# Feed-forward blocks of four pairs of chunks in a fused block-attention and FFN kernel, with rooms in SBUF shared anew

## Chip, cores and metric

The kernel runs on one core of a Trainium2 chip. The metric is the device time of one execution in microseconds (us). Before the change the median of three runs is 938.62 us (938.25 to 939.14), so differences under about 0.2% (1.9 us) can't be told from no change.

## What is computed

Queries, keys and values are float32 of 8 batches, 8 heads, 576 positions and 64 values per head. A sequence is cut into 9 chunks of 64 positions, and a chunk attends to itself alone. The result, laid out as 4608 tokens of 512 values, goes through a feed-forward network (FFN) with a squared ReLU:

```python
scores = scale * np.matmul(q_c, k_c.transpose(0, 1, 2, 4, 3))
scores = scores - np.max(scores, axis=-1, keepdims=True)
attn = np.exp(scores)
attn = attn / (np.sum(attn, axis=-1, keepdims=True) + 1e-09)
out = np.matmul(attn, v_c)
...
h = x @ w_in
r = np.maximum(h, 0.0)
g = r * r
return (g @ w_out).astype(np.float32)
```

The weights (512 by 2048 and 2048 by 512) arrive as float64, as pairs of 32-bit words.

## The kernel before, in words

**Values in two parts.** Every float32 value that a large matrix product uses is split into a high part, which fits the type fp32r, and a low part, the rest. A product is then three matmuls: high times high, high times low, low times high. In the FFN the names are `xh`, `xl` (tokens), `wi` (first weights), `gh`, `gl` (squared ReLU) and `wo` (second weights).

**Pairs, units and blocks.** A pair is two neighbouring chunks, 128 tokens; there are 36. A unit is one pair with four of the eight heads, so there are 72 units, two to a pair (unit u belongs to pair u // 2). Pairs are grouped into FFN blocks by the list `blocks` (line 63): one of four pairs, ten of three, one of two. For a block of n pairs the FFN goes in 16 steps f, one for each 128 of the 2048 hidden values. A step has 12 matmuls into the PSUM tile `h` (`mm_in`, L623: four quarters of the 512 inputs, three matmuls each, moving operand n*128 wide), then `act` (ReLU on ACT, square on DVE, high part on ACT, low part on DVE), and, two steps later (`LAG`), three matmuls for each pair into the PSUM tiles `o` (`mm_out`, L667, moving operand 512 wide). The accumulators `o` of a block are taken in turn from four PSUM banks. At a block's end each is copied to an SBUF tile `ob` (two buffers) and stored.

**Attention of the late pairs.** The first 8 pairs (`NN`) are done in the first stage by other code, while the weights are converted. Each of the other 28 goes through these steps, for a pair or for its two units:
- `load_qk`: 16 DMAs bring q and k of a pair into the tiles `q_raw` and `k_raw`, one buffer each. `transpose_pair` (L284) turns them on DVE into `qt` and `kt` and then calls for the next pair's load.
- `stack_qk` (L297): the high part of q goes to the tile `qst` on ACT (L306), the low part to a tile `ql` on DVE (L308), and a DMA on each half copies it into the other half of `qst` (L310). High and low parts of k go to `kst` (L312, L316), with two DMAs (L314). `qst` and `kst` have one buffer each.
- `s2`: four matmuls `sc` (L353) into two PSUM tiles, copied by ACT and added by DVE (L363, L365) to `e`; then maximum, difference, exponential. `norm` divides by the sum.
- `s3`: two transposes `pt` on PE (L403), then `pst` on ACT (L417), two DMAs (L419) and the low parts on DVE (L421).
- `load_v` and `stack_v`: four DMAs of 64 by 8 by 64 values bring v of a whole pair into two tiles `v_raw` (L278, two buffers in all); ACT and POOL split each unit's part into `vs` (L331, L334). After the pair's second unit the next pair's v is called for.
- `s4`: four matmuls `xt` (L437) into two PSUM tiles, whose sums `x` become columns of `xh` and `xl` (L449 to L457).

`sc`, `pt` and `xt` share two PSUM banks in turn.

**What sets the order.** All DMAs of the late pairs and the stores are issued by SP, one after the other; an issue that has to wait holds up those behind it. The order on PE is written out in lines 935 to 959: the matmuls and `act` calls of a block (`ops`) are cut into as many equal pieces as there are slots, and `merge` spreads a slot's attention steps over its piece. Slot t holds `s2` of unit t-1, `s4` of t-3, `stack_v` of t-2, `norm` of t-1, `transpose_pair` and `stack_qk` for unit t if it opens a pair, and `s3` of t-2. Block 1 (the second) also opens the late tiles and has two slots without attention first; then its slots run from t = 16 until the pairs of block 2 are through. Any later block's slots bring the pairs of the block behind it. The other engines' order is set by a scheduler from the order of the code and priorities.

**The first stage.** `first_block` lists the work of block 0, the conversion of the weights and the attention of pairs 0 to 7 with costs, and a small planner (`Plan`) sorts it. Pair 7 belongs to block 2 there, whose `xh` and `xl` use the room of block 0's, so its result is placed by `place(NN - 1)` at the end of the stage. The copies `kt` of these pairs lie in the pool `nat`.

Of the kernel before, what the change touches and what calls it, by code (L numbers as in the profile page):

```python
# [10 lines left out]
F32 = mybir.dt.float32  # L11
F32R = mybir.dt.float32r
# [8 lines left out]
def kernel(  # L21
# [24 lines left out]
    P = 128  # L46
# [13 lines left out]

    ABUFS = 3
    PRIO = 300
    blocks = [4] + [3] * 10 + [2]
    LAG = 2
    HEAD = 1
    REST = 0
# [7 lines left out]
    XB = (max(blocks[::2]), max(blocks[1::2]))  # L74


    NN = sum(blocks[:2]) + 1
    first_pair = [sum(blocks[:b]) for b in range(len(blocks))]

    const = ctx.enter_context(tc.tile_pool(name="const", bufs=1))  # L80
# [29 lines left out]
    def open_late():  # L110

        early.close()
        pool = ctx.enter_context(tc.tile_pool(name="late", bufs=2))
        late["pool"] = pool
        late["q"] = pool.tile([P, H, 2, CH], F32R, name="qst", tag="qst", bufs=1)
        late["p"] = pool.tile([P, 2, HP, 2, 2, CH], F32R, name="pst", tag="pst", bufs=1)
        load_v(NN)
        nc.gpsimd.memset(late["p"].bitcast(F32), 0.0)
        late["k"] = pool.tile([P, 2, 2, H, CH], F32R, name="kst", tag="kst", bufs=1)
        for c in range(2):  # L120
            r = slice((1 - c) * CH, (2 - c) * CH)
            nc.gpsimd.memset(late["k"].bitcast(F32)[r, 1, c], 0.0)
# [133 lines left out]
                        s = src[bb, :, i0:i0 + 32, dh * 32:(dh + 1) * 32]  # L256
                        nc.sync.dma_start(out=t[r0:r0 + 32, :, ih, :], in_=s.rearrange("h i d -> i h d"))

    def load_v(pair):


        if pair < NN:
            for c in range(2):
                bb, n0 = divmod(2 * pair + c, NCH)
                for h2, r in enumerate(halves):
                    s = v[bb, h2:H:2, n0 * CH:(n0 + 1) * CH, :]
                    nc.sync.dma_start(
                        out=vbd[slot_of(pair)][r, :, c, h2, :], in_=s.rearrange("h i d -> i h d")
                    )
            return  # L270
        pairs[pair]["v"] = []
        for c in range(2):
            t = late["pool"].tile([P, H, D], F32, name=f"v_raw{pair}_{c}", tag="v_raw")
            pairs[pair]["v"].append(t)
            bb, n0 = divmod(2 * pair + c, NCH)
            s = v[bb, :, n0 * CH:(n0 + 1) * CH, :].rearrange("h i d -> i h d")
            for r in halves:
                nc.sync.dma_start(out=t[r], in_=s)  # L278

# [17 lines left out]
    def stack_qk(pair):  # L297

        qt, kt = pairs[pair]["q"], pairs[pair]["k"]
        kst = late["k"]
        qst = late["q"]
        low = late["pool"].tile([P, H, CH], F32R, name=f"ql{pair}", tag="kk", bufs=1)
        for c, (own, oth) in enumerate(other):
            nc.scalar.copy(qst[own, :, c], qt[own])  # L306
        for c, (own, oth) in enumerate(other):
            nc.vector.tensor_tensor(low[own], qt[own], qst.bitcast(F32)[own, :, c], op=ALU.subtract)  # L308
        for c, (own, oth) in enumerate(other):
            nc.sync.dma_start(out=qst.bitcast(F32)[oth, :, c], in_=low.bitcast(F32)[own])  # L310
        for c, (own, oth) in enumerate(other):
            nc.scalar.copy(kst[own, 0, c], kt[own])  # L312
        for c, (own, oth) in enumerate(other):
            nc.sync.dma_start(out=kst.bitcast(F32)[oth, 0, c], in_=kst.bitcast(F32)[own, 0, c])  # L314
# [8 lines left out]
    def stack_v(u):  # L323


        b, pair, j, hq = units[u]
        vs = late["pool"].tile([P, 2, HP, 2, D], F32R, name=f"vs{u}", tag="vs")
        ust[u]["v"] = vs
        for c, t in enumerate(pairs[pair]["v"]):
            vr = t[:, hq * HQ:(hq + 1) * HQ].rearrange("p (a b) d -> p a b d", b=2)  # L330
            nc.scalar.copy(vs[:, c], vr)  # L331
            for h2, r in enumerate(halves):
                dst = (r, slice(None), 1 - h2)
                nc.gpsimd.tensor_tensor(  # L334
                    vs[:, c][dst], vr[dst], vs.bitcast(F32)[:, c][dst], op=ALU.subtract
                )
        if hq == NQ - 1 and pair + 1 < NPAIR:
            load_v(pair + 1)

    def s2(u):  # L340

# [145 lines left out]
    class Pair:  # L487
# [26 lines left out]
            copy(qbd[self.u % 2][r, :, s], self.psq[r])  # L514

        def keep_k(self):
            self.kt = nat.tile([P, H, CH], F32, name=f"kt{self.u}", tag=f"kt{self.u % 2}")
            nc.scalar.copy(self.kt, self.psk)

        def scores(self):  # L520
# [261 lines left out]
    def first_block():  # L782
# [29 lines left out]
                add(e, 2 * ISSUE, lambda n=n: load_one(u, n), writes=[("qk"[n], u)], size=P * DM * 4)  # L812

        def load_values(u):
            add(SP, 4 * ISSUE, lambda: load_v(u), writes=[("v", slot_of(u))], size=P * DM * 4)

        def attention(u):
            x = prs[u]
            i = u % 2
            if x.lead:  # L820
                bq, bk, bs = ("o", 2 * i), ("o", 2 * i + 1), ("h", i)
            else:
                bq, bk, bs = (("at", next(turn_at) % 2) for _ in range(3))
# [18 lines left out]
            if u < NN - 1:
                place(u)

        def place(u):
            x = prs[u]
            j = u if u < NN - 1 else 0
            bx = x.banks["xt"]
            add(ACT, ONE, lambda: x.place(0), [bx], [("xh", j)])
            add(DVE, TWO, lambda: x.place(1), [bx, ("xh", j)], [("xl", j)])  # L850
# [60 lines left out]
        for n in range(got, n_items):  # L911
# [5 lines left out]
                u += 1  # L917
            fetch(n)
            convert(n)
        add(SP, 16 * ISSUE, lambda: load_qk(NN), writes=["late"], size=2 * P * DM * 4)  # L920
        for f in range(NF):
            p.rank = NN + n_items
            ffn_in(f)
# [1 line left out]
                ffn_out(f - LAG)  # L925
            p.rank = -1
            square(f)
        place(NN - 1)
        p.run()

    with tc.manual_schedule(engines={PE, DVE, ACT, SP, POOL}):
# [59 lines left out]
```

## Time and profile before

| | before |
|---|---|
| device time, median of 3 runs | 938.62 us |
| span of the profiled execution, first to last instruction | 936.9 us |
| device time of that execution itself | not given beside its span; the median above is 1.7 us longer than the span |
| PE busy with matmuls | 920.5 us (98%), 5018 instructions |
| PE busy with weight loads | 825.2 us (88%) |
| DVE, ACT, POOL busy | 75%, 63%, 23% |
| TensorE clock granted, mean | 0.998 |
| moved by DMA | 85.01 MB, 91 GB/s |

A row of a view names an engine, the source line, the operation and its tiles. SPq is SP's queue: a row there is the issue of a DMA, and its time that of the issue and not of the transfer. Matmuls overlap, so the duration of one is longer than the step from one to the next; the chain of waits shows the steps.

### The profile page before, as it was taken

To read this page: it belongs to the slowest core of one execution; us is meant where nothing else is said; L and a number is where in the kernel's file an instruction comes from. 1 tells how busy PE (TensorE), PEld (TensorE's weight loads), DVE (VectorE), ACT (ScalarE), POOL (GpSimd) and SP (SyncE) were. 2 spreads that over 40 slices of the span, in tenths; PEclk is the share of its full clock that TensorE was granted. 3 is DMA by queue.
4 is the path that set the end of the run, shared out by engine and by line. 5 is a ranking of instruction groups with operands and counts; after the bars stand their busy time and mean duration, and the time that the engine had idled before them with its cause. 6 is when DMAs were issued, how large, how long until landed. Compare 5 with 4: busy or idle time off the path is not lost.

```text
span 936.9 us, 16741 instructions
## 1 busy us (share of the span) xinstructions
PE 920.5 (98%) x5018; PEld 825.2 (88%) x5018; DVE 698.3 (75%) x1607; ACT 592.5 (63%) x1463; POOL 212.1 (23%) x351
## 2 busy tenths in 40 slices
PE   8899999999999999999999999999999999999998
PEld 8788878888899999999999999999989999998997
DVE  5989995788778877877877877877787877753332
ACT  5788875576666666766766766766666666653332
POOL 2000002043222233333322222333333222221000
PEclk9999999999999999999999999999999999999999
DMA  9875505444444543543433543444543442210000
GB/s 197 249 189 175 190 14 121 80 84 103 95 79 76 113 76 76 111 77 74 106 70 71 112 76 67 109 76 79 113 80 75 88 104 57 57 40 12 1 34 23
DMA packets 287193, 85.01 MB, mean 91 GB/s; under 512 B 268672, under 2 KB 276864, under 8 KB 287104
## 3 DMA queue, kind: packets, MB, share of 16 engines
q1 hardware_dynamic: 284992, 83.42, 40.8%
q8 instruction: 41, 0.67, 0.3%
q10 hardware_dynamic: 2112, 0.52, 0.3%
q14 instruction: 48, 0.39, 0.1%
HBM read 52.43 MB, written 9.44 MB: 66 GB/s over the span
## 4 chain that ended last, share of the span: by engine, by line
PE 89%; DVE 6%; DMA 2%; ACT 1%; issue 1%; DVEq 0%; ACTq 0%; SPq 0%
PE h L623 40%; PE o L667 39%; PE sc L353 3%; PE xt L437 3%; PE pt L403 1%; PE sc L527 1%; PE xt L581 1%; DMA kst<-kst 1%; DMA qk_raw<-in_k_dram 0%; DVE gl L650 0%; DVE wia L177 0%; PE k L503 0%; DVE woa L177 0%; ACT qst L306 0%; DVE nz L548 0%
## 5 line engine op out<-in xcount | busy, mean ns | idle before, releaser
L623 PE MATMUL h<-xh,wi 128*128 128x384 f32 (+2 forms) x1536 | 433.7, 339 | 1.8 <-DVE wi L198 1.5
L667 PE MATMUL o<-wo,gh 128*128 128x512 f32 x1152 | 371.7, 396 | 0.0
L623 PEld LDWEIGHTS h<-xh,wi 128*128 128x128 f32 x1536 | 275.0, 188 | 16.0 <-DVE wi L198 1.9
L623 PE MATMUL h<-xl,wi 128*128 128x384 f32 (+2 forms) x768 | 260.5, 339 | 1.2 <-DVE xl L594 1.2
L667 PEld LDWEIGHTS o<-wo,gh 128*128 128x128 f32 x1152 | 208.2, 188 | 33.0
L667 PE MATMUL o<-wo,gl 128*128 128x512 f32 x576 | 226.5, 393 | 0.0
L334 POOL TENSOR_TENSOR vs<-v_raw,vs 64x128 fp32r<-64x128 f32 x224 | 115.8, 517 | 241.4 <-ACT vs L331 227.5
L650 DVE TENSOR_TENSOR gl<-g,gh 128x384 fp32r<-128x384 f32 (+2 forms) x192 | 111.0, 578 | 64.3 <-ACT gh L647 60.5
L623 PEld LDWEIGHTS h<-xl,wi 128*128 128x128 f32 x768 | 144.7, 188 | 8.2 <-DVE xl L594 1.6
L638 DVE TENSOR_TENSOR g<-g 128x384 f32<-128x384 f32 (+1 forms) x176 | 98.5, 560 | 67.5 <-ACT g L634 66.0
L647 ACT CAST gh<-g 128x384 fp32r<-128x384 f32 (+2 forms) x192 | 98.5, 513 | 76.7 <-PE o L667 52.2
L634 ACT ACTIVATE g<-h 128x384 f32<-128x384 f32 (+2 forms) x192 | 94.5, 492 | 79.2 <-PE h L623 57.9
L667 PEld LDWEIGHTS o<-wo,gl 128*128 128x128 f32 x576 | 108.2, 188 | 20.7
L390 POOL TENSOR_TENSOR e<-e,z 128x256 f32<-128x256 f32 x56 | 45.3, 810 | 229.4 <-DVE z L389 66.7
L365 DVE TENSOR_TENSOR e<-sc,e 64x128 f32<-64x128 f32 x224 | 64.7, 289 | 34.4 <-ACT e L363 29.7
L363 ACT COPY e<-sc 64x128 f32<-64x128 f32 x224 | 58.2, 260 | 42.5 <-PE sc L353 39.2
L451 DVE TENSOR_TENSOR x<-xt,x 64x128 f32<-64x128 f32 x224 | 64.6, 289 | 22.3 <-ACT x L449 17.9
L449 ACT COPY x<-xt 64x128 f32<-64x128 f32 x224 | 58.1, 259 | 35.1 <-PE xt L437 31.7
L353 PE MATMUL sc<-kst,qst 128*128 128x256 f32 x224 | 62.9, 281 | 2.0 <-DVE pst L421 1.1
L437 PE MATMUL xt<-pst,vs 128*128 128x256 f32 x224 | 62.7, 280 | 1.8 <-DMA pst<-pst 1.3
L457 POOL TENSOR_TENSOR xl<-x,xh 128x256 fp32r<-128x256 f32 x56 | 44.2, 790 | 59.7 <-ACT xh L456 57.5
L421 DVE TENSOR_TENSOR pst<-pt,pst 64x256 fp32r<-64x256 f32 x112 | 47.3, 422 | 11.0 <-ACT pst L417 7.0
(80 smaller groups left out, 898.1 us busy)
## 6 DMA issues: line engine op xcount, KB each, us to landing
v_raw<-in_v_dram SPq DMA_DIRECT2D x112, 128.0 KB, 3.3
out_dram<-ob SPq DMA_DIRECT2D x36, 256.0 KB, 2.1
wiraw<-in_moe_w_in_dram SPq DMA_DIRECT2D x16, 512.0 KB, 6.1
woraw<-in_moe_w_out_dram SPq DMA_DIRECT2D x16, 512.0 KB, 6.0
q_raw<-in_q_dram SPq DMA_DIRECT2D x224, 32.0 KB, 2.1
k_raw<-in_k_dram SPq DMA_DIRECT2D x224, 32.0 KB, 2.1
qst<-ql SPq DMA_DIRECT2D x56, 128.0 KB, 2.6
kst<-kst SPq DMA_DIRECT2D x56, 128.0 KB, 2.6
```

The costliest lines, as they stand in the source:

```text
L334: nc.gpsimd.tensor_tensor(vs[:, c][dst], vr[dst], vs.bitcast(F32)[:, c][dst], op=ALU.subtract)
L353: nc.tensor.matmul(ps.rearrange("p w c j -> p (w c j)"), late["q"][:, hh].rearrange("p c i -> p (c i)"), late["k"][:, :, :, hh], start=Tru ...
L363: nc.scalar.copy(e[r], ps[r, :, 1, c])
L365: nc.vector.tensor_tensor(e[r], ps[r, :, 0, c], e[r], op=ALU.add)
L437: nc.tensor.matmul(st["xt"][hp][:, c].rearrange("p w a q -> p (w a q)"), st["v"][:, c, hp].rearrange("p a d -> p (a d)"), late["p"][:, :, ...
L451: nc.vector.tensor_tensor(x[r, hp], ps[hp][r, :, 0, h2], x[r, hp], op=ALU.add)
L623: nc.tensor.matmul(self.h[:, :self.n], a[:, c], bb[:, c, :self.n], start=c == 0 and i == 0, stop=c == NCC - 1 and i == 2,)
L634: nc.scalar.activation(self.g, self.h[:, :self.n], AF.Relu)
L638: nc.vector.tensor_tensor(self.g, self.g, self.g, op=ALU.mult)
L647: nc.scalar.copy(self.gh[:, :self.n], self.g)
L650: nc.vector.tensor_tensor(self.gl[:, :self.n], self.g, self.gh.bitcast(F32)[:, :self.n], op=ALU.subtract)
L667: nc.tensor.matmul(acc[b, j], a[:, j * P:(j + 1) * P], bb, start=f == 0 and i == 0, stop=f == NF - 1 and i == 2,)
```

## The change

`blocks` becomes nine blocks of four pairs. So `mm_in` is always 512 wide, and there are 9 * 16 * 12 = 1728 of them in place of 2304; `mm_out` stays at 1728. `NN` stays 8, now exactly two blocks, so pair 7 belongs to block 1, which has rooms of its own, and is placed like the pairs before it. Block 1 has 13 pieces (two without attention, then t = 16 to 26) where it had 9 (t = 16 to 22); a later block has 8 slots where it had 6.

The `xh` and `xl` of the odd blocks need more room. It comes from three edits. The low part of q is written into `qt` itself, and the DMAs to `qst` read `qt`; the tile `ql` is gone. v of a late pair is loaded for one unit at a time (`load_v(u)`, four DMAs of half the size, issued after the split of the unit before), so a pair takes eight such DMAs. `kt` of the early pairs lies in the rooms of `q_raw` and `k_raw`, and the first late load waits for its last readers.

```diff
-    blocks = [4] + [3] * 10 + [2]
+    blocks = [4] * 9
...
-    NN = sum(blocks[:2]) + 1
+    NN = sum(blocks[:2])
...
-        load_v(NN)
+        load_v(NQ * NN)
...
+    def load_v(u):
+
+
+        b, pair, j, hq = units[u]
+        ust[u]["vraw"] = []
         for c in range(2):
-            t = late["pool"].tile([P, H, D], F32, name=f"v_raw{pair}_{c}", tag="v_raw")
-            pairs[pair]["v"].append(t)
+            t = late["pool"].tile([P, HQ, D], F32, name=f"v_raw{u}_{c}", tag="v_raw")
+            ust[u]["vraw"].append(t)
+            bb, n0 = divmod(2 * pair + c, NCH)
+            s = v[bb, hq * HQ:(hq + 1) * HQ, n0 * CH:(n0 + 1) * CH, :].rearrange("h i d -> i h d")
             for r in halves:
                 nc.sync.dma_start(out=t[r], in_=s)
...
-        low = late["pool"].tile([P, H, CH], F32R, name=f"ql{pair}", tag="kk", bufs=1)
...
-            nc.vector.tensor_tensor(low[own], qt[own], qst.bitcast(F32)[own, :, c], op=ALU.subtract)
+            nc.vector.tensor_tensor(qt[own], qt[own], qst.bitcast(F32)[own, :, c], op=ALU.subtract)
         for c, (own, oth) in enumerate(other):
-            nc.sync.dma_start(out=qst.bitcast(F32)[oth, :, c], in_=low.bitcast(F32)[own])
+            nc.sync.dma_start(out=qst.bitcast(F32)[oth, :, c], in_=qt[own])
...
-        if hq == NQ - 1 and pair + 1 < NPAIR:
-            load_v(pair + 1)
+        if u + 1 < NU:
+            load_v(u + 1)
...
-            self.kt = nat.tile([P, H, CH], F32, name=f"kt{self.u}", tag=f"kt{self.u % 2}")
+            self.kt = raw.tile([P, H, CH], F32, name=f"kt{self.u}", tag="qk"[self.u % 2] + "_raw")
...
-        add(SP, 16 * ISSUE, lambda: load_qk(NN), writes=["late"], size=2 * P * DM * 4)
+        add(SP, 16 * ISSUE, lambda: load_qk(NN), writes=[("kt", 0), ("kt", 1)], size=2 * P * DM * 4)
...
-        place(NN - 1)
```

The change moves instructions on every engine. First SP's queue in block 1, in the middle of its attention slots. Before, from the qst and kst copies of one late pair (tile names count up through the program) to those of the next:

```order
L310 DMA qst<-ql_2214 64x8x64
L314 DMA kst<-kst 64x512
L257 DMA q_raw_2457<-in_q_dram 32x8x32
L278 DMA v_raw_0_2330<-in_v_dram 64x8x64 x2
L278 DMA v_raw_1_2333<-in_v_dram 64x8x64
L419 DMA pst<-pst 64x4x64 x2
L278 DMA v_raw_1_2333<-in_v_dram 64x8x64
L257 DMA q_raw_2457<-in_q_dram 32x8x32 x7
L257 DMA k_raw_2466<-in_k_dram 32x8x32 x7
L419 DMA pst<-pst 64x4x64 x2
L257 DMA k_raw_2466<-in_k_dram 32x8x32
L310 DMA qst<-ql_2477 64x8x64
```

After the change, the same stretch of SP's queue, for a pair in the same block:

```order
L312 DMA qst<-qt_2118 64x8x64 x2
L316 DMA kst<-kst 64x512 x2
L281 DMA v_raw_0_2242<-in_v_dram 64x4x64 x2
L421 DMA pst<-pst 64x4x64 x2
L281 DMA v_raw_1_2245<-in_v_dram 64x4x64 x2
L257 DMA q_raw_2358<-in_q_dram 32x8x32 x8
L257 DMA k_raw_2367<-in_k_dram 32x8x32
L281 DMA v_raw_0_2341<-in_v_dram 64x4x64 x2
L421 DMA pst<-pst 64x4x64 x2
L281 DMA v_raw_1_2344<-in_v_dram 64x4x64 x2
L257 DMA k_raw_2367<-in_k_dram 32x8x32 x7
L312 DMA qst<-qt_2354 64x8x64 x2
```

Between two pairs' first qst copies stand 28 issues before (four of qst and kst, 16 of q and k, four of v, four of pst) and 32 now (eight of v).

Second, DVE at the same place. Before, from the second low part of a pair's q (L308) to the transpose of the next pair's q into the one tile `qt` (L284):

```order
L308 TENSOR_TENSOR ql_2214<-qt_2190,qst 64x512
L650 TENSOR_TENSOR gl_10_2134<-g_10_2130,gh_10_2133 128x384
L372 TENSOR_TENSOR e_2112<-e_2112,m_2139 128x256
L316 TENSOR_TENSOR kst<-kt_2192,kst 64x512
L284 STREAM_TRANSPOSE qt_2453<-q_raw_2194 128x512
```

After:

```order
L310 TENSOR_TENSOR qt_2118<-qt_2118,qst 64x512
L318 TENSOR_TENSOR kst<-kt_2120,kst 64x512
L374 TENSOR_TENSOR e_2040<-e_2040,m_2058 128x256
L318 TENSOR_TENSOR kst<-kt_2120,kst 64x512
L453 TENSOR_TENSOR x_2070<-xt_0_2064,x_2070 64x128 x2
L652 TENSOR_TENSOR gl_7_2086<-g_7_2082,gh_7_2085 128x512
L453 TENSOR_TENSOR x_2070<-xt_1_2077,x_2070 64x128 x2
L287 STREAM_TRANSPOSE kt_2356<-k_raw_2131 128x512
L389 TENSOR_REDUCE z_2059<-e_2040 128x4
L287 STREAM_TRANSPOSE qt_2354<-q_raw_2122 128x512
```

The transpose into `qt` has moved behind that of k and stands ten operations behind the low part instead of three; it overwrites what the DMAs to qst read.

Third, PE at the end of the attention, where no `sc` is left: from the last `pt` of unit 70 to the first `xt` that uses it. Before:

```order
L403 MATMUL pt_10374<-ident,e_10053 128x128
L623 MATMUL h_7_10368<-xl_9176,wi_931 128x384
L623 MATMUL h_7_10368<-xh_9175,wi_931 128x384
L667 MATMUL o_0_10159<-wo_872,gh_5_10315 128x512 x2
L667 MATMUL o_0_10159<-wo_872,gl_5_10316 128x512
L667 MATMUL o_1_10163<-wo_872,gh_5_10315 128x512 x2
L667 MATMUL o_1_10163<-wo_872,gl_5_10316 128x512
L667 MATMUL o_2_10180<-wo_872,gh_5_10315 128x512 x2
L437 MATMUL xt_0_10398<-pst,vs_10346 128x256
```

After, for the same unit:

```order
L405 MATMUL pt_9546<-ident,e_9324 128x128
L669 MATMUL o_2_8931<-wo_1184,gh_9_9442 128x512 x2
L669 MATMUL o_2_8931<-wo_1184,gl_9_9443 128x512
L669 MATMUL o_3_8937<-wo_1184,gh_9_9442 128x512 x2
L669 MATMUL o_3_8937<-wo_1184,gl_9_9443 128x512
L439 MATMUL xt_0_9564<-pst,vs_9523 128x256
```

Ten FFN matmuls stood between the two, and six now. For unit 71, the last, 17 stood there, and ten now.

More of the change, by code (lines that the diff above doesn't have):

```diff
@@ L257, in load_qk, with load_lead_v @@
                         nc.sync.dma_start(out=t[r0:r0 + 32, :, ih, :], in_=s.rearrange("h i d -> i h d"))
[L259 to L271, printed above, removed]
+    def load_lead_v(pair):
         for c in range(2):
-            t = late["pool"].tile([P, H, D], F32, name=f"v_raw{pair}_{c}", tag="v_raw")
-            pairs[pair]["v"].append(t)
             bb, n0 = divmod(2 * pair + c, NCH)
-            s = v[bb, :, n0 * CH:(n0 + 1) * CH, :].rearrange("h i d -> i h d")
+            for h2, r in enumerate(halves):
+                s = v[bb, h2:H:2, n0 * CH:(n0 + 1) * CH, :]
+                nc.sync.dma_start(
+                    out=vbd[slot_of(pair)][r, :, c, h2, :], in_=s.rearrange("h i d -> i h d")
+                )
+    def load_v(u):
+        b, pair, j, hq = units[u]
+        ust[u]["vraw"] = []
+        for c in range(2):
+            t = late["pool"].tile([P, HQ, D], F32, name=f"v_raw{u}_{c}", tag="v_raw")
+            ust[u]["vraw"].append(t)
+            bb, n0 = divmod(2 * pair + c, NCH)
+            s = v[bb, hq * HQ:(hq + 1) * HQ, n0 * CH:(n0 + 1) * CH, :].rearrange("h i d -> i h d")
             for r in halves:
@@ L323, in stack_v @@
     def stack_v(u):
-        b, pair, j, hq = units[u]
+        st = ust[u]
         vs = late["pool"].tile([P, 2, HP, 2, D], F32R, name=f"vs{u}", tag="vs")
-        ust[u]["v"] = vs
-        for c, t in enumerate(pairs[pair]["v"]):
-            vr = t[:, hq * HQ:(hq + 1) * HQ].rearrange("p (a b) d -> p a b d", b=2)
+        st["v"] = vs
+        for c, t in enumerate(st["vraw"]):
+            vr = t.rearrange("p (a b) d -> p a b d", b=2)
             nc.scalar.copy(vs[:, c], vr)
@@ L814, in load_values @@
         def load_values(u):
-            add(SP, 4 * ISSUE, lambda: load_v(u), writes=[("v", slot_of(u))], size=P * DM * 4)
+            add(SP, 4 * ISSUE, lambda: load_lead_v(u), writes=[("v", slot_of(u))], size=P * DM * 4)
         def attention(u):
@@ L841, in attention @@
             add(PE, 16 * 0.11 + w, x.values, [("v", slot_of(u)), "tt"], [bx])
[L842 to L850, printed above, removed]
+            add(ACT, ONE, lambda: x.place(0), [bx], [("xh", u)])
+            add(DVE, TWO, lambda: x.place(1), [bx, ("xh", u)], [("xl", u)])
         def convert(n):
```

## The prediction

> **What bounds the kernel now.** I read the page first, then the busy time by windows, the chain of waits, SP's queue and the waits of PE. The page says that PE has work nearly all the time at nearly full clock:
>
> ```profile
> span 936.9 us, 16741 instructions
> ...
> PE 920.5 (98%) x5018; PEld 825.2 (88%) x5018; DVE 698.3 (75%) x1607; ACT 592.5 (63%) x1463; POOL 212.1 (23%) x351
> ...
> PEclk9999999999999999999999999999999999999999
> ...
> PE 89%; DVE 6%; DMA 2%; ACT 1%; issue 1%; DVEq 0%; ACTq 0%; SPq 0%
> ```
>
> So only two things can move the time: the step from one matmul to the next, and the little idle time of PE. The windows show where that idle time lies (length, then busy time of PE, weight loads, DVE, ACT, POOL):
>
> ```profile
> 180.00:200.00 20.00, 17.96 (x97) 15.73 (x96) 17.82 (x46) 14.11 (x40) 6.80 (x11) 1.00 0.42 74
> 200.00:220.00 20.00, 18.47 (x98) 15.46 (x97) 17.02 (x43) 14.12 (x40) 6.92 (x13) 1.00 0.49 92
> 220.00:240.00 20.00, 19.57 (x106) 17.51 (x105) 15.64 (x39) 13.26 (x36) 5.46 (x9) 1.00 0.47 107
> 240.00:260.00 20.00, 19.74 (x107) 17.69 (x106) 15.64 (x40) 12.41 (x36) 7.35 (x12) 1.00 0.49 93
> 260.00:333.70 73.70, 73.70 (x397) 66.94 (x396) 58.21 (x142) 48.98 (x130) 21.83 (x36) 1.00 0.43 86
> ```
>
> From 260 us on a block of three pairs takes 73.7 us with no idle time on PE, and DVE is free a fifth of it. From 180 to 260, in block 1 and just behind it, PE idles 2.04 + 1.53 + 0.43 + 0.26 = 4.3 us, and DVE is busy up to 89%: there the attention limits PE. Block 1 brings its pairs at a faster pace than any later block.
>
> **The matmuls, on the path throughout.** The chain of waits gives the steps: start, length and count.
>
> ```profile
> 133.46 2.72 PE o L667 x12
> ...
> 159.75 2.10 PE h L623 x12
> ...
> 270.67 0.12 PE sc L353
> ...
> 339.80 2.08 PE o L667 x9
> ...
> 902.34 1.43 PE h L623 x12
> ```
>
> A 512-wide matmul takes 2.72 / 12 = 0.227 us in a long run of its like, and 2.08 / 9 = 0.231 where other widths come between. A 384-wide one takes 2.10 / 12 = 0.175, a 256-wide one 1.43 / 12 = 0.119. By the column these are 0.44 to 0.45, 0.456 and 0.465 ns, so wide matmuls are hardly cheaper, and the 576 that go away carry their columns over.
>
> From block 1 on `mm_in` has now 1920 * 0.175 + 192 * 0.119 = 358.8 us and `mm_out` 1536 * 0.231 = 354.8, together 713.6. After the change there are 3072, all 512 wide. 2688 of them lie in blocks 1 to 7, where attention matmuls (0.12 us) come between every few; I take 0.231 for these, the row from such a place. Block 8 has no attention beside it: 384 at 0.227. That is 620.9 + 87.2 = 708.1, a gain of **5.5 us**. If all ran at 0.227 it would be 16.3; at 0.231 throughout, 4.0.
>
> The Trainium skill, "TensorE: Matmul & The Clock Gate", section "Back-to-back issue gap", gives a warm step of N / 2.4 ns and 2.5 ns more. By it the 576 fewer matmuls would save 576 * 2.5 ns = 1.4 us, an estimate, and the sum would be 4.1 us higher. This trace has another fixed part: 0.119, 0.175 and 0.227 us lie 12 to 15 ns above N / 2.4.
>
> **Block 1, the attention's pace.** The FFN of block 1 is cut into 9 pieces before, into 13 after. A piece has (1920 / 10 * 0.175 + 144 * 0.231) / 9 = 7.4 us of FFN before and 384 * 0.231 / 13 = 6.8 after. A unit's ten attention matmuls add 10 * 0.12 = 1.2. So a pair, two units, has 17.2 us on PE before and 16.0 after; in later blocks 24.6 in both (73.7 / 3). Against this stands what SP must issue for a pair. One cycle of SP's queue in block 1 (rows of SPq: start, time of the issues, count):
>
> ```profile
> 196.49 0.61 SPq L314 DMA_DIRECT2D kst<-kst  x1
> ...
> 201.10 1.32 SPq L419 DMA_DIRECT2D pst<-pst  x2
> 202.47 0.62 SPq L278 DMA_DIRECT2D v_raw<-in_v_dram  x1
> 203.14 4.29 SPq L257 DMA_DIRECT2D q_raw<-in_q_dram  x7
> 207.53 3.41 SPq L257 DMA_DIRECT2D k_raw<-in_k_dram  x7
> 211.04 1.29 SPq L419 DMA_DIRECT2D pst<-pst  x2
> 212.38 0.59 SPq L257 DMA_DIRECT2D k_raw<-in_k_dram  x1
> 214.23 0.59 SPq L310 DMA_DIRECT2D qst<-ql  x1
> ```
>
> From 201.10 to 212.97 SP issues 20 DMAs without a pause, 0.594 us each. A pair has 28, 16.6 us: just under the 17.2 on PE, and SP is not yet the limit (it waits from 212.97 to 214.23 for its data). The change makes them 32. Half a load of v is no cheaper to issue than a whole one, as the early loads of that size show beside the late ones:
>
> ```profile
> 79.95 2.61 SPq L267 DMA_DIRECT2D vbd<-in_v_dram  x4
> ...
> 243.56 2.68 SPq L278 DMA_DIRECT2D v_raw<-in_v_dram  x4
> ```
>
> So a pair takes SP 32 * 0.594 = 19.0 us, 3.0 more than PE. Since q and k of the next pair and both units' v stand ahead of the qst and kst copies, and PE's `sc` needs these, PE waits. Block 1 now runs to t = 26: it goes from pair 8's copies to pair 13's, and four of these cycles (9 to 13) are full, 4 * 3.0 = 12.0 us. The first is bound, as before, by the chain through ACT and DVE; I leave it 1.4 of the 4.3 us (a third of what three pairs lost). Together 13.4 in place of 4.3: a loss of **9.1 us**. DVE's groups (busy us, mean ns) and one 512-wide low part say what it has to do besides:
>
> ```profile
> L638 DVE TENSOR_TENSOR g<-g 128x384 f32<-128x384 f32 x17 | 9.6, 567 | 3.9 <-ACT g L634 3.7
> L650 DVE TENSOR_TENSOR gl<-g,gh 128x384 fp32r<-128x384 f32 x16 | 9.3, 581 | 4.0 <-ACT gh L647 3.8
> ...
> 143.95 0.69 DVE L650 TENSOR_TENSOR gl<-g,gh 128x512 fp32r<-128x512 f32 x1
> ...
> 194.28 0.59 SPq L310 DMA_DIRECT2D qst<-ql  x1
> ```
>
> A late pair costs DVE (58.21 - 16 * 1.15) / 3 = 13.3 us; with 2.5 steps of 1.4 us it has 16.8 of each 19, so it agrees with a cycle of that length and does not lengthen it.
>
> Bounds: if SP's issues hide as now, nothing is lost beyond the 4.3, a term of 0. A gain I exclude: the pace gets faster, and nothing on ACT or DVE gets shorter by a pair. If the waits that SP has now in a cycle (214.23 back to the qst of the cycle before it, 194.28, the last row here, less 16.6, so 3.4 us) come on top of its 19.0, it is 4 * 6.4 + 1.4 - 4.3 = 22.7.
>
> In later blocks 19.0 of 24.6 us leave SP room, and I cost the halved loads at nothing there; without that room each pair would cost what SP lacks.
>
> **The end of the attention.** PE waits once for the copies of `pst`:
>
> ```profile
> PE xt L437 <- DMA pst<-pst: 1.3, 1, 1.3
> ...
> 845.41 0.12 PE pt L403
> ...
> 849.04 0.36 PE xt L437
> ```
>
> From the last `pt` to the `xt` that uses it the copies need 3.63 us. The order now has six matmuls there for unit 70, 0.11 + 6 * 0.231 = 1.5 us, so a wait of 2.1; ten for unit 71, 2.4 us, a wait of 1.2. In place of 1.3 that is a loss of **2.0 us** (0 if the copies land sooner in the emptier queue, 4 if both wait in full).
>
> **The rest, at nothing.** Placing pair 7 earlier puts one operation each of 0.6 to 0.7 us on ACT and DVE ahead of the last weights, and takes one away behind them; 0 to 0.7. The first late load waits for the last `kt`, long before its data is used. Four stores at a block's end share two buffers; the `o` bank is wanted again only after the 12 `mm_in` and nine `mm_out` that follow, 21 * 0.231 = 4.9 us, which covers a store; 0 to 2 in all. Writing q's low part in place costs the same DVE operations, but the next transpose into `qt` must wait for the landing:
>
> ```profile
> qst<-ql SPq DMA_DIRECT2D x56, 128.0 KB, 2.6
> ```
>
> It stands ten operations behind, some 5 us at the durations above, against 2.6 and an issue or two of 0.6: hidden as long as SP issues at once.
>
> **The sum.** -5.5 + 9.1 + 2.0 = +5.6 us, so a span of 942.5. The span lies 1.7 us under the median of the runs; with that, **944.2 us**.
>
> **The rivals.**
> 1. SP does not limit block 1. For it: from block 2 on the same queue runs with room, SP does wait 1.3 us in the cycle shown, and the loads stand a pair ahead, so the qst copies could go out when their data is ready. Against it: 19.0 over 16.0. Decided by whether SP still idles before the qst issues. Then -5.5 + 0 + 2.0 = -3.5: 935.1 us, faster. The Trainium skill, "DMA: Bandwidth & Descriptors", section "Issuing engines are not separate DMA queues", has the rule for this case: the sequencer's time to initiate a DMA "is usually small relative to the DMA itself". This trace speaks against it for such small loads: 0.6 us of every issue is SP's, and the queue is full for 12 us on end.
> 2. The 512-wide matmuls run at 0.227 even between attention matmuls, since the switch between 384 and 512 is what costs now. For it: block 0's long runs. Against it: the 0.231 row stands among attention matmuls too. Then -16.3 + 9.1 + 2.0 = -5.2: 933.4 us.
> 3. Held in line: SP is late everywhere, the transpose into `qt` waits for late qst copies, and DVE stands with everything behind it, in later blocks too. It decides when SP is later by more than the 15.5 us that DVE has free in 73.7 allow, 5 us a pair. At 1 us beyond that in 20 pairs, 964 us. Against it: SP's 5.6 us of room a pair.
>
> **Chances.** The forecast's mechanism has 0.62 with the waits up to its upper bound, of which 0.05 come out within 0.2% of now; rival 1 has 0.25, of which 0.10 come out the same (a part of the wait stays); rival 2 has 0.09; rival 3 has 0.04. So slower by over 0.2% (1.9 us, about what a measurement of this kernel can tell from no change) 0.61, the same 0.15, faster 0.24. The range reaches down to a little under rival 1, 934, and up to 954, short of the full upper bound of the block 1 term (957.8).
>
> **What would show it.** In the profile after: steps of 0.231 in blocks 1 to 7 and 0.227 in block 8; PE idle some 13 us between 170 and 260 us, ended by DMAs to kst or by DVE operations behind them; SPq without a pause there, with qst copies some 19 us apart; two waits of `xt` for `pst` at the end; later blocks of some 98 us without idle time. Wrong it would be if qst copies come 16 us apart in block 1, or PE waits in blocks 2 to 7.

## The result: 972.3 us in place of 938.9, and the profile after

The changed kernel takes 972.34 us (median of four runs, 969.59 to 974.93), the kernel before 938.88 beside it: 1.035 times the time, 95% interval 1.0327 to 1.0372. The forecast was 944.2 with a range up to 954: the sign was right, the size was not.

The page of the changed kernel, the lines that answer to those shown of before:

```profile
span 969.9 us, 15518 instructions
...
PE 925.5 (95%) x4442; PEld 755.8 (78%) x4442; DVE 690.0 (71%) x1516; ACT 575.6 (59%) x1362; POOL 199.3 (21%) x351
...
PE 56%; DVE 17%; ACT 8%; issue 7%; DMA 7%; SPq 3%; POOL 1%; DVEq 0%; ACTq 0%; POOLq 0%
```

PE has 576 matmuls fewer but is busy for no less time, and of the chain that ended last only 56% is PE's own work, where it was 89%. So the time went into waits. The windows say where they lie (length, then busy time of PE, weight loads, DVE, ACT, POOL, then the granted clock):

```profile
180.00:200.00 20.00, 18.24 (x88) 14.16 (x87) 17.67 (x43) 14.31 (x39) 6.96 (x12) 1.00 0.47 88
200.00:220.00 20.00, 16.11 (x76) 12.41 (x75) 17.17 (x43) 13.94 (x37) 7.59 (x13) 0.98 0.49 91
220.00:240.00 20.00, 16.99 (x76) 13.05 (x74) 15.17 (x38) 13.30 (x35) 6.35 (x11) 0.93 0.45 86
240.00:260.00 20.00, 16.71 (x80) 13.12 (x80) 16.82 (x43) 13.97 (x37) 7.00 (x12) 1.00 0.48 91
...
400.00:500.00 100.00, 97.75 (x461) 79.36 (x460) 76.70 (x177) 62.65 (x161) 25.74 (x48) 1.00 0.43 85
```

From 180 to 260 us PE idles 12.0 us, where it was 4.3. And from 290 to 800 us it idles some 2.4 us in every 100, where it had no idle time at all. The waits of PE name what ended them (total us, times, longest). The first row is of before, the others are of the changed kernel:

```profile
PE sc L353 <- DVE pst L421: 1.1, 3, 0.5
```

```profile
PE sc L355 <- DVE pst L423: 14.3, 22, 1.8
PE sc L355 <- DVE z L391: 6.1, 2, 3.2
PE sc L355 <- DMA kst<-kst: 4.3, 3, 1.8
PE xt L439 <- DMA pst<-pst: 3.8, 3, 2.0
```

The largest is one wait: `sc` of the next unit needs the PSUM bank that `pt` holds until DVE has taken the low parts `pst` out of it, and DVE comes to that too late.

Idle time is not the whole price of a wait, since a matmul overlaps the one before it. So I also counted every matmul from its start to the next one's, beyond the usual step of its width (0.231, 0.175, 0.119 us). By that count PE lost 6.1 us in block 1 (160 to 290 us) before and 23.0 after; 0.2 before and 17.2 after from 290 to 800; 1.6 before and 5.1 after from 800 to 870. That is 37.4 us more; less the 5.5 that the matmul steps were forecast to give, 31.9 of the 33.0 by which the span grew.

### The profile page after: what moved, and what is told of

Same layout as the page of the kernel before. It is cut to its first block, busy times and chain, and to the rows that moved or that the text cites. A ratio compares the mean times of both kernels' runs of the same rounds, so it can differ in the third digit from the quotient of the medians.

```text
span 969.9 us, 15518 instructions
## 1 busy us (share of the span) xinstructions
PE 925.5 (95%) x4442; PEld 755.8 (78%) x4442; DVE 690.0 (71%) x1516; ACT 575.6 (59%) x1362; POOL 199.3 (21%) x351
## 4 chain that ended last, share of the span: by engine, by line
PE 56%; DVE 17%; ACT 8%; issue 7%; DMA 7%; SPq 3%; POOL 1%; DVEq 0%; ACTq 0%; POOLq 0%
PE h L625 26%; PE o L669 24%; DVE x L453 3%; PE sc L355 2%; SPq L257 2%; ACT qst L308 2%; DVE pst L423 2%; ACT g L636 2%; DMA out_dram<-ob 2%; DVE gl L652 2%; DMA kst<-kst 2%; DVE qt L287 2%; PE xt L439 2%; DMA qst<-qt 1%; DVE z L390 1%
## 5 line engine op out<-in xcount | busy, mean ns | idle before, releaser
L625 PE MATMUL h<-xh,wi 128*128 128x512 f32 x1152 | 393.7, 397 | 1.5 <-ACT wi L189 1.1
L625 PEld LDWEIGHTS h<-xh,wi 128*128 128x128 f32 x1152 | 213.8, 190 | 45.1 <-ACT wi L189 1.5
L625 PE MATMUL h<-xl,wi 128*128 128x512 f32 x576 | 228.1, 396 | 1.3 <-DVE xl L596 1.3
L640 DVE TENSOR_TENSOR g<-g 128x512 f32<-128x512 f32 x128 | 92.3, 721 | 94.0 <-ACT g L636 93.0
L636 ACT ACTIVATE g<-h 128x512 f32<-128x512 f32 x144 | 86.2, 598 | 108.1 <-PE h L625 68.1
L652 DVE TENSOR_TENSOR gl<-g,gh 128x512 fp32r<-128x512 f32 x144 | 99.2, 689 | 48.8 <-ACT gh L649 47.5
L649 ACT CAST gh<-g 128x512 fp32r<-128x512 f32 x144 | 89.2, 619 | 61.2 <-PE o L669 55.4
L625 PEld LDWEIGHTS h<-xl,wi 128*128 128x128 f32 x576 | 109.2, 190 | 20.2 <-DVE xl L596 1.7
L392 POOL TENSOR_TENSOR e<-e,z 128x256 f32<-128x256 f32 x56 | 34.8, 621 | 235.0 <-DVE z L391 87.3
L355 PEld LDWEIGHTS sc<-kst,qst 128*128 128x128 f32 x224 | 42.6, 190 | 44.0 <-issue 33.4
```

Of the source, the lines that this page charges most:

```text
L355: nc.tensor.matmul(ps.rearrange("p w c j -> p (w c j)"), late["q"][:, hh].rearrange("p c i -> p (c i)"), late["k"][:, :, :, hh], start=Tru ...
L625: nc.tensor.matmul(self.h[:, :self.n], a[:, c], bb[:, c, :self.n], start=c == 0 and i == 0, stop=c == NCC - 1 and i == 2,)
L636: nc.scalar.activation(self.g, self.h[:, :self.n], AF.Relu)
L640: nc.vector.tensor_tensor(self.g, self.g, self.g, op=ALU.mult)
L649: nc.scalar.copy(self.gh[:, :self.n], self.g)
L652: nc.vector.tensor_tensor(self.gl[:, :self.n], self.g, self.gh.bitcast(F32)[:, :self.n], op=ALU.subtract)
```

## Experiments

Three theories came first. *Queue*: SP's longer list of issues delays the scores. *In line*: the 512-wide operations of the feed-forward part on ACT and DVE hold up `pst`. *In place*: writing q's low part into `qt` moves the transposes behind other work on DVE. Others came as these fell. All runs, with the idle time of PE in three windows of the profiled execution (length of the window less PE's busy time; the profiled executions of 7 and 10 lie some 4 us below their medians, that of 11 5 us above):

| kernel | median us | ratio to before (95%) | PE idle 160-290 | 290-800 | 800-870 |
|---|---|---|---|---|---|
| before | 938.9 | 1 | 4.3 | 0.0 | 1.3 |
| changed | 972.3 | 1.035 (1.033-1.037) | 16.9 | 12.2 | 3.1 |
| 1 before, low part in place | 947.6 | 1.009 (1.007-1.010) | 5.1 | 2.7 | 1.3 |
| 2 before, v by units | 938.8 | 0.9995 (0.998-1.001) | 4.8 | 0.3 | 1.3 |
| 3 changed, later blocks of three | 963.6 | 1.025 (1.023-1.028) | 15.1 | 3.6 | 2.3 |
| 4 changed, v issued by POOL | 951.1 | 1.013 (1.011-1.014) | 10.7 | 2.1 | 3.1 |
| 5 changed, no 1e-9 | 973.0 | 1.036 (1.034-1.038) | 17.9 | 13.5 | 3.2 |
| 6 as 1, no 1e-9 | 944.9 | 1.005 (1.004-1.007) | 5.1 | 1.6 | 1.3 |
| 7 changed, `ql` back | 959.7 | 1.021 (1.018-1.023) | 15.0 | 2.9 | 3.1 |
| 8 changed, one head piece less | 972.1 | 1.035 (1.032-1.038) | 14.9 | 11.2 | 3.1 |
| 9 changed, `xl` zero | 960.3 | 1.022 (1.020-1.023) | 16.3 | 4.3 | 3.1 |
| 10 changed, 4 and 7 together | 957.0 | 1.018 (1.016-1.021) | 13.2 | 2.2 | 3.1 |
| 11 as 10, mixed blocks | 949.2 | 1.012 (1.010-1.015) | 5.6 | 8.8 | 3.1 |
| 12 as 11, refill first | 994.1 | 1.058 (1.057-1.060) | 9.0 | 31.4 | 6.1 |
| 13 as 7, mixed blocks, late `xt` | 945.6 | 1.007 (1.005-1.008) | 3.7 | 8.2 | 0.0 |
| 14 before, faster block 1 | 942.6 | 1.004 (1.003-1.005) | 7.4 | 0.3 | 1.3 |
| 15 before, late `xt` | 937.5 | 0.998 (0.997-0.999) | 5.4 | 0.0 | 0.0 |

**1 and 2: one part of the change alone, on the kernel before.**

```diff
-            nc.vector.tensor_tensor(low[own], qt[own], qst.bitcast(F32)[own, :, c], op=ALU.subtract)
+            nc.vector.tensor_tensor(qt[own], qt[own], qst.bitcast(F32)[own, :, c], op=ALU.subtract)
...
-            nc.sync.dma_start(out=qst.bitcast(F32)[oth, :, c], in_=low.bitcast(F32)[own])
+            nc.sync.dma_start(out=qst.bitcast(F32)[oth, :, c], in_=qt[own])
```

> The kernel before with one part of the change alone: q's low part is written into qt in place, blocks and v loads as before. Three theories of the 33 us are set against each other. Queue theory: SP's longer list of issues delays the scores, in block 1 above all. In-line theory: the 512-wide feed-forward operations on ACT and DVE hold up pst, so that PE waits 0.75 us a pair in blocks 2 to 7. In-place theory: the transposes into qt move behind others on DVE, and that makes the 0.75 us a pair. Queue and in-line theory expect no change here: 937 to 941 us. The in-place theory expects 0.5 to 0.8 us for each of some 25 pairs: 950 to 960 us.

> The kernel before with another part of the change alone: v of a late pair is loaded for one unit at a time, so that a pair has 32 issues on SP instead of 28. Queue theory: in block 1 a cycle of SP becomes 19 to 21 us against 17.2 of PE, over about three cycles; 5 to 12 us more, 944 to 951 us, all of it in block 1. In-line and in-place theory: 937 to 941 us.

The second edit is that of the change (`load_v(u)`). Measured: 947.6 and 938.8 us. The edit in place costs 8 us by itself, most of it as waits at `sc` from block 2 on, where I had costed it at nothing; the halved loads of v cost nothing at the kernel before's pace. Queue theory fell here for that pace; in place came out at about half its price, 0.3 us a pair.

**3: the changed kernel with three pairs a block from block 3 on.**

```diff
-    blocks = [4] * 9
+    blocks = [4] * 3 + [3] * 8
```

> The changed kernel with blocks 3 onward of three pairs ([4] * 3 + [3] * 8), all other edits kept; block 1 is as in the changed kernel. By the widths alone the sum goes up 8 * 192 * 0.175 - (5 * 192 * 0.231 + 192 * 0.227) = 3.4 us. In-line theory: the waits of 0.75 us a pair go away where the blocks are of three, 20 pairs, 15 us: 972.3 - 15 + 3.4 = 961 us. Queue and in-place theory: the waits in later blocks stay, 976 us.

963.6 us, near the in-line theory's 961. But the waits of later blocks do not all go: 3.6 us of idle time stay, about as many as in experiment 1. So the 512-wide operations make a wait that comes from the edit in place more than twice as long (12.2 us of idle time from 290 to 800 with them, 3.6 without).

**7: q's low part in a tile of its own again**, which shares the room of the results `ob`.

```diff
+        low = gp.tile([P, H, CH], F32R, name=f"ql{pair}", tag="o")
...
-            nc.vector.tensor_tensor(qt[own], qt[own], qst.bitcast(F32)[own, :, c], op=ALU.subtract)
+            nc.vector.tensor_tensor(low[own], qt[own], qst.bitcast(F32)[own, :, c], op=ALU.subtract)
```

> The changed kernel with the in-place edit undone: q's low part has a tile of its own again, which shares the two buffers of the stored results ob. Blocked addition: the transposes and z return to their old order, z no longer meets POOL, and the waits of blocks 2 to 7 go: 955 to 960 us. Block 1, if the queue of SP sets it, keeps its 23 us. In-line theory: 968 to 974 us.

959.7 us, at the upper edge of what was expected, with the 512-wide operations unchanged. The waits of PE in this kernel: the one that led the list is all but gone.

```profile
PE sc L356 <- DMA kst<-kst: 8.6, 6, 2.4
...
PE sc L356 <- DVE pst L424: 1.6, 6, 0.3
```

**What the moved transposes run into.** Around one wait of the changed kernel, first DVE, then POOL, then PE (start, length, operation, idle time before it):

```profile
410.68 0.59 DVE L453 TENSOR_TENSOR x<-xt,x 64x128 f32<-64x128 f32 x2
411.30 0.71 DVE L287 STREAM_TRANSPOSE qt<-q_raw 128x512 f32<-128x512 f32 x1
411.94 0.68 DVE L390 TENSOR_SCALAR z<-z 128x4 f32<-128x4 f32 x1
412.52 0.68 DVE L652 TENSOR_TENSOR gl<-g,gh 128x512 fp32r<-128x512 f32 x1
...
413.93 0.69 DVE L640 TENSOR_TENSOR g<-g 128x512 f32<-128x512 f32 x1 [0.64 <-ACT g L636]
414.65 0.86 DVE L423 TENSOR_TENSOR pst<-pt,pst 64x256 fp32r<-64x256 f32 x2
...
411.85 0.73 POOL L459 TENSOR_TENSOR xl<-x,xh 128x256 fp32r<-128x256 f32 x1 [0.61 <-ACT xh L458]
...
414.88 0.40 PE L625 MATMUL h<-xh,wi 128*128 128x512 f32 x1
415.66 0.36 PE L355 MATMUL sc<-kst,qst 128*128 128x256 f32 x1 [0.38 <-DVE pst L423]
```

The addition of 1e-9 to four sums a partition (L390) takes 0.68 us: it starts while POOL works on `xl` and ends at 412.62, just behind POOL's end at 412.58. Everything behind it on DVE is late by as much: `gl`, with it the release of the one buffer `g`, the ReLU on ACT that waits for `g` and stands ahead of `pst`, the square, and `pst`. PE goes from one start to the next in 0.78 us instead of 0.231. In the groups (busy us, mean ns) the addition is seen to have more than doubled; the first row is of before, the second of the changed kernel:

```profile
L388 DVE TENSOR_SCALAR z<-z 128x4 f32<-128x4 f32 x56 | 9.6, 171 | 0.7
```

```profile
L390 DVE TENSOR_SCALAR z<-z 128x4 f32<-128x4 f32 x56 | 20.3, 362 | 1.0
```

Before, the transpose of q stood further ahead, and `gl` was done when POOL began with `xl`, as these rows of DVE and POOL in the kernel before show. No addition took longer than 0.3 us there; in the changed kernel 21 of the 56 take more than 0.4.

```profile
564.17 0.56 DVE L650 TENSOR_TENSOR gl<-g,gh 128x384 fp32r<-128x384 f32 x1
564.64 0.16 DVE L388 TENSOR_SCALAR z<-z 128x4 f32<-128x4 f32 x1
...
564.72 0.73 POOL L457 TENSOR_TENSOR xl<-x,xh 128x256 fp32r<-128x256 f32 x1 [1.00 <-ACT xh L456]
```

**5 and 6: without the addition** (both leave out the 1e-9).

```diff
-            nc.vector.tensor_scalar_add(z, z, 1e-9)
```

> The changed kernel without one operation of 4 values a partition: the addition of 1e-9 to the sums z (line 390) is left out; nothing else moves in DVE's order. In the traces this small DVE operation takes 0.17 us, but 0.68 where it starts while POOL computes xl: it ends 25 ns behind POOL's operation. That is so 21 times in the changed kernel, once a pair from block 2 on, and never before the change. New theory, the blocked addition: the in-place edit moves the transposes in DVE's order behind z, z then meets POOL's xl, and the 0.5 us that it loses is the wait of PE at sc in blocks 2 to 7. It expects the waits there to fall from 17 us to 3 or less: 955 to 960 us; block 1 as it is. In-line theory (the 512-wide operations): the waits lose only the 0.17 us that the operation itself takes, 968 to 972 us.

> The kernel before with q's low part in place, which alone took 947.6 us, and without the addition of 1e-9 to z. Blocked addition: the 0.3 us a pair of blocks 2 and later go, and the time is that of the kernel before, 938 to 941 us. If the moved transposes themselves hold up pst, by their 1.4 us: 946 to 948 us.

973.0 and 944.9 us: the theory that the addition alone is the culprit fell (944.9 lies between what its two sides expected). The rows of DVE and POOL in experiment 5, at the same place, show why:

```profile
414.33 0.14 DVE L390 RECIPROCAL z<-z 128x4 f32<-128x4 f32 x1
414.39 1.14 DVE L651 TENSOR_TENSOR gl<-g,gh 128x512 fp32r<-128x512 f32 x1
...
414.25 0.74 POOL L458 TENSOR_TENSOR xl<-x,xh 128x256 fp32r<-128x256 f32 x1 [0.60 <-ACT xh L457]
```

Now `gl`, which reads two tiles of SBUF, takes the blow: 1.14 us in place of 0.68. The Trainium skill, "SBUF — State Buffer", section "Who interferes with whom", has the rule: a VectorE operation with two SBUF inputs, or a `tensor_scalar` in its two-port mode, and a GpSimd operation that reads SBUF shut each other out, and whichever starts second waits for the other's end. The rows agree: 414.25 + 0.74 is 414.99, and 0.54 us later `gl` is done.

**9: POOL does not read.** The low parts `xl` of the late pairs are left out; DVE's order stays.

```diff
-            nc.gpsimd.tensor_tensor(xl[dst], src, xh.bitcast(F32)[dst], op=ALU.subtract)
+            nc.gpsimd.memset(xl.bitcast(F32)[dst], 0.0)
```

> The changed kernel with the low parts xl of the late pairs left out: POOL fills them with zeros (an operation that reads nothing from SBUF and comes earlier) instead of subtracting. DVE's order stays as it is, with the transposes behind x and z. The addition of 1e-9 alone was not it: without it, the next operation with two inputs in SBUF, gl, took 1.15 us instead of 0.69 while POOL computed xl. Lock theory, widened: whatever DVE operation with two SBUF inputs, or tensor_scalar, comes behind the transpose waits till POOL's xl is done; without POOL's reading the waits at sc in blocks 2 to 7 go, 17 us less: 955 to 958 us. Order theory: the 1.4 us of transposes ahead of pst are the loss, whatever POOL does: 968 to 972 us.

960.3 us, 12 us less than the changed kernel and much nearer to the lock theory than to the order theory. DVE at the same place:

```profile
411.44 0.71 DVE L287 STREAM_TRANSPOSE qt<-q_raw 128x512 f32<-128x512 f32 x1
412.07 0.13 DVE L390 TENSOR_SCALAR z<-z 128x4 f32<-128x4 f32 x1
412.11 0.68 DVE L652 TENSOR_TENSOR gl<-g,gh 128x512 fp32r<-128x512 f32 x1
```

Same order, and z is back at 0.13. So some 12 of the 17 us of blocks 2 to 7 are shown to need both: they go with the old order (7, median 12.6 us lower), and they go without POOL's read (9, 12.1 lower). What makes the other 5, in either kernel, is not shown.

In one thing the expectation of 7 was wrong: `z` still meets POOL there, in 21 of the 56 additions. Its rows of DVE, POOL and PE at the like place:

```profile
406.80 0.69 DVE L653 TENSOR_TENSOR gl<-g,gh 128x512 fp32r<-128x512 f32 x1
407.41 0.70 DVE L391 TENSOR_SCALAR z<-z 128x4 f32<-128x4 f32 x1
...
408.94 0.86 DVE L424 TENSOR_TENSOR pst<-pt,pst 64x256 fp32r<-64x256 f32 x2
...
407.35 0.74 POOL L460 TENSOR_TENSOR xl<-x,xh 128x256 fp32r<-128x256 f32 x1 [0.98 <-ACT xh L459]
...
409.98 0.32 PE L356 MATMUL sc<-kst,qst 128*128 128x256 f32 x1
```

So the loss of 0.5 us to POOL alone costs PE next to nothing: `gl` stands ahead of `z` and releases `g` in time, and `pst` is done at 409.80, ahead of the `sc` at 409.98. In the changed kernel the loss and the moved transpose (0.71 us) both lie between `x` and `pst`. Either alone fits into the margin at most pairs (7 and 9), the two together do not.

**4 and 10: v issued by POOL's queue**, alone and together with the tile `ql`.

```diff
             for r in halves:
-                nc.sync.dma_start(out=t[r], in_=s)
+                nc.gpsimd.dma_start(out=t[r], in_=s)
```

> The changed kernel with the late loads of v issued by POOL's queue instead of SP's, so that a pair has 24 issues on SP (24 * 0.594 = 14.3 us, less than the 16.0 that PE has for a pair in block 1). Queue theory: block 1's 23 us of waits fall to some 6 as before the change, 955 us; the qst copies of block 1 come some 16 us apart; blocks 2 to 7 as they are. If SP is not what limits block 1: 970 to 975 us, and qst copies still 20 us apart.

> The changed kernel with both remedies: q's low part in a tile of its own, and v issued by POOL. If the two cure the same 13 us of blocks 2 to 7 by two ways, and only the second relieves block 1 (by 9 us), the gains don't add up: 972.3 - 13 - 9 = 950 us, about that of v on POOL alone (951.1). If they are independent: 972.3 - 12.7 - 21.3 = 938 us.

951.1 us, more than the queue theory promised, and for another reason too. Idle time in block 1 falls from 16.9 to 10.7 us, not to 4.3, and the cycles there (start of one pair's `qst` copies to the next) from 19.0 to 21.6 us down to 17.5 to 19.3. But the waits of later blocks go as well. POOL and DVE of experiment 4 say why:

```profile
376.27 2.44 POOL L281 DMA_DIRECT2D v_raw<-in_v_dram  x4
378.77 0.89 POOL L459 TENSOR_TENSOR xl<-x,xh 128x256 fp32r<-128x256 f32 x1
...
376.98 0.13 DVE L390 TENSOR_SCALAR z<-z 128x4 f32<-128x4 f32 x1
377.02 0.68 DVE L652 TENSOR_TENSOR gl<-g,gh 128x512 fp32r<-128x512 f32 x1
```

The four issues, 0.61 us each, stand ahead of `xl` on POOL, so `xl` runs 2 us later and misses z and this `gl`. Together with the tile `ql`, 957.0 us: both remedies cure the same waits, as expected, but the sum is 6 us over v on POOL alone. The idle times explain 2.6 of it, all in block 1; the rest, which the profiled executions do not show, stays open.

**8, 11, 12, 13, 14: block 1.** With `HEAD = 0` (8) the block has 12 pieces, with `HEAD = 2` in the kernel before (14) ten.

```diff
-    HEAD = 1
+    HEAD = 0
```

> The changed kernel with block 1 cut into 12 pieces instead of 13 (HEAD = 0: one piece without attention at its start instead of two). A piece is then 7.4 us of feed-forward work, a pair 17.2 us on PE, as it was before the change. If the cycle of 20 to 21 us in block 1 is set by something else than PE (SP's queue or the chain through ACT and DVE), each of five cycles hides 1.2 us more of it, and the time falls by about 6 us to 966 us, with qst copies still 20 us apart. If the cycle shrinks or grows with PE's work: 970 to 974 us.

972.1 us: no gain. The copies of `qst` come as in the changed kernel, 17.7 to 22.1 us apart, and begin at the same time: at 158.39, where the changed kernel has them at 158.14. The attention can't start earlier, and PE waits for the first `kst` instead, once 7.4 us. So slowing the pace this way only moves the wait.

```diff
-    HEAD = 1
+    HEAD = 2
```

> The kernel before with one line changed: HEAD = 2, so block 1 is cut into 10 pieces instead of 9 and a pair has 2 * (66.6 / 10 + 1.2) = 15.7 us on PE there instead of 17.2, with 28 issues a pair on SP. Pace theory: the cycle stays at 17.8 to 20 us, and the waits of block 1 grow from 6.1 to 9 to 12 us; the attention also begins one piece later; 941 to 945 us. Queue theory: 28 issues are 15.4 to 16.6 us, about the pace, and little is lost: 938 to 941 us.

942.6 us, 3.6 more than before, with nothing changed but the pace of block 1 and, with it, the piece at which its attention starts: idle time 7.4 in place of 4.3, cycles of 19.1 and 20.7 us against 15.7 of PE. As the pace theory had it.

```diff
-    blocks = [4] * 9
+    blocks = [4, 4, 3, 3, 3, 3, 4, 4, 4, 4]
```

> Both remedies, and blocks [4, 4, 3, 3, 3, 3, 4, 4, 4, 4]: block 1 is still of four pairs, but has the attention of three pairs beside it instead of four, cut into 11 pieces. A pair then has 2 * (88.7 / 11 + 1.2) = 18.5 us on PE in block 1, as long as the 18.6 to 19.3 us of a cycle with v on POOL. If that cycle is a floor set by the refill of qst and kst through ACT, DVE and the DMA, the waits of block 1 fall from 14 us to some 5: by the widths -4 us against the kernel before, waits about as before, 935 to 940 us. If the pace is not the cause: 947 to 951 us.

> As the one before, and the copies and splits that refill qst and kst go ahead of other work on ACT and DVE (raised priority). If the refill's length sets the cycle of block 1, the waits at sc fall further, by 0.5 to 1 us for each of four pairs: 2 to 4 us less than without. If it only pushes other work back: no change, or up to 3 us more.

949.2 us (11): block 1's idle time falls from 13.2 to 5.6, as expected, but 8.8 us come up in later blocks, some 5 of them from 450 to 600 us, where the last block of three has four pairs beside it. That v's issues on POOL make them is not borne out: experiment 13, with v on SP, has 8.2 us there, some 5 in the same stretch. The raised priority (12) costs 45 us: `xt` waits for DVE's `e` 39.1 us in 24 waits. Pushing one chain ahead starves the other.

Experiment 13 has these blocks and the tile `ql`, with v on SP, 32 issues a pair, and empty steps in the place of the missing `sc`:

```diff
             if lo <= t - lag < hi:
                 yield from stage(t - lag)
+            elif t > hi:
+                yield from [lambda: None] * (HQ + HQ // 2 + 1) if stage is s2 else ()
```

> The changed kernel with q's low part in a tile of its own, the mixed blocks [4, 4, 3, 3, 3, 3, 4, 4, 4, 4] as in the run before, v back on SP's queue (32 issues a pair), and the last slots without sc filled up with empty steps, so that 18 and 22 feed-forward matmuls stand between the pt and the xt of units 70 and 71 instead of 6 and 10. Block 1, if the pace alone made its loss: waits of some 7 us as with v on POOL. If SP's 32 issues matter too (17.4 to 18.1 us of SP's time against 18.5 of PE): 10 to 14 us. Blocks 2 to 8: below 1 us of waits in 100 as with the tile of its own and v on SP. End of attention: no wait of xt for pst, 3.6 us less. Together 942 to 949 us.

945.6 us. The windows of block 1:

```profile
180.00:200.00 20.00, 18.44 (x88) 14.73 (x87) 17.73 (x41) 13.94 (x37) 4.68 (x9) 1.00 0.48 88
200.00:220.00 20.00, 19.47 (x93) 15.04 (x91) 17.09 (x42) 14.36 (x39) 6.37 (x12) 1.00 0.45 82
220.00:240.00 20.00, 18.86 (x90) 14.65 (x89) 16.91 (x42) 14.09 (x37) 6.74 (x13) 1.00 0.48 91
240.00:260.00 20.00, 19.52 (x103) 16.96 (x102) 15.66 (x41) 12.53 (x34) 7.83 (x12) 1.00 0.55 129
```

3.7 us idle in these four, as little as before the change, with all 32 issues on SP. The cycles are no shorter (19.2 to 21.1 us); PE just has 18.5 us of work in each. So block 1 of the changed kernel lost its 17 us because a cycle takes longer than the work beside it: four full cycles of 20.4 us on average against 16.0 of PE's work for each make 17.6. In later blocks the expectation missed: below 1 us of waits in 100 was expected, and the 8.2 us are more.

**15: only the spacing at the end, on the kernel before** (the same two lines as in 13).

> The kernel before with the last slots filled up with empty steps, so that more feed-forward matmuls stand between pt and xt of the last two units. The 1.5 us that xt waits there should go: 937.4 us against 938.9, a version faster than both kernels, by as much as can just be told. If the wait only moves to the start of the last block, no change.

937.5 us, ratio 0.9984 (0.9974 to 0.9993): the wait goes (idle 0.0 from 800 to 870) and nothing takes its place. This is the fastest version of the study, by a difference that can just be told from none.

## Why the prediction was wrong, step by step

**The matmul steps: right.** In the chain a stretch in block 3 has six `o` in 1.39 us, 0.232 each, and block 8 has 2.72 us for twelve, 0.227:

```profile
424.91 1.39 PE o L669 x6
...
880.48 2.72 PE o L669 x12
```

**The step that failed: "The rest, at nothing".** I asked of the edit in place whether the transpose into `qt` would have to wait for the copies, found ten operations of cover, and stopped: "hidden as long as SP issues at once". From 290 us on no transpose waited (in block 1 DVE stood 0.6 us for these copies, once). What the ten operations meant was the other way round: the transpose of q had moved behind the sum of z and `x`, so z and `gl` came when POOL reads `x`, and lost 0.5 us to it once a pair. The margin between `pt` and the next `sc` was too small for the moved transpose and this loss together, smaller still with 512-wide operations (experiments 1, 3, 7 and 9). Price: 17 us in place of 0, of which some 12 are shown to come this way. The prediction had named "PE waits in blocks 2 to 7" as a sign of being wrong, and that is what came. The order of DVE's rows was in the document; I read from it who waits, and not what then runs beside POOL.

**Block 1: the direction right, the size too small, the limit named only in part.** 23.0 us in place of 6.1, a term of 16.9 where I put 9.1 (the upper bound of 22.7 covered it). The forecast of SP's list was close: 32 issues took 17.4 to 18.1 us, or 19.4 to 20.0 with the short pauses between them, against the 19.0 that I put (its 0.594 us an issue has such pauses in it). But the cycles were 19.0 to 21.6 us (the shortest has 29 issues), since SP also has to wait within it, 0.6 to 2.2 us in those of 32, for POOL's split of v above all. Rows of SP's queue in one cycle of the changed kernel:

```profile
214.00 1.34 SPq L312 DMA_DIRECT2D qst<-qt  x2
...
224.95 0.45 SPq L257 DMA_DIRECT2D k_raw<-in_k_dram  x1
227.55 0.60 SPq L281 DMA_DIRECT2D v_raw<-in_v_dram  x1
...
231.67 3.78 SPq L257 DMA_DIRECT2D k_raw<-in_k_dram  x7
235.56 1.34 SPq L312 DMA_DIRECT2D qst<-qt  x2
```

SP waits 2.15 us here, from 225.40 to 227.55. I took SP as the limit; with v off SP the cycle is still 17.5 to 19.3 us against 16.0 (experiment 4), and with all of v on SP but a slower pace the loss is gone (experiment 13). So the loss is what the work of PE falls short of the cycle, and SP's list is one limit of the cycle with another close behind it. What SP's part is worth, in idle time of block 1: 2 us from experiment 7 to 10, 6 from the changed kernel to experiment 4. What sets the cycle of 18 us without SP, the refill of `qst` and `kst` through ACT, DVE and the copies, was argued from the chain and not shown by itself.

**The end of the attention: the mechanism right, the size too small.** The two waits of `xt` came where the order put them, 2.2 and 1.3 us against 2.1 and 1.2. Not foreseen was a lower clock behind the first (below), 1.5 us, and 0.9 us at one more `xt` at 784 us.

**The rivals.** The first two (SP not the limit, wide matmuls cheaper) would have made it faster, and neither did: SP counts for something, and the steps stayed at 0.231 to 0.232 in blocks 1 to 7. The third, held in line in later blocks too, had the right place and about the right price, 964 us, and I gave it 0.04. Its mechanism was another: from 290 us on no transpose waited for SP. I ruled it out because SP had room, and looked for no other way in which DVE's line could be held up.

## What to carry to other kernels

An edit that only saves a buffer adds a dependency, and a scheduler answers with another order: look at what then meets on DVE and POOL, and how much margin is left, not only at whether the new wait is covered. A stage whose cycle is set by a chain through several engines loses what the pace of the work beside it falls short of, so count the work that each block brings for a cycle before changing block sizes. Where the last steps of a software pipeline lack one stage, keep its place empty, so that the distances in the stages that remain stay as they were.

## What the hardware showed beside this

A DVE operation that meets POOL's reading can lose the rest of POOL's operation: z went from 0.17 to 0.68 us, `gl` from 0.68 to 1.14. Those that read PSUM, the transposes and the reductions kept their times: two `x` took 0.59 us while POOL split v at 410.68, the transposes 0.70 and the reductions of z 0.42, as elsewhere.

After a wait the granted clock fell for some microseconds. In the changed kernel, rows of the chain and a window behind the wait of `xt`:

```profile
843.72 2.15 DMA pst<-pst
...
847.42 3.40 PE h L625 x8
```

```profile
845.00:855.00 10.00, 8.99 (x34) 7.35 (x35) 2.67 (x7) 2.56 (x7) 0.36 (x1) 0.83 0.04 8
```

Eight matmuls took 0.425 us each instead of 0.231, at a mean clock of 0.83: a wait of 2.2 us cost 1.5 us more. In two of block 1's windows above it was 0.98 and 0.93, so a part of the 23.0 is of this kind. It comes behind some waits and not behind others; what decides was not tried.
